# Cosine attention and a gated product: bank rotation of the projection, an earlier first projection, and held norms

## The chip, the cores and the metric

The kernel runs on one core of a Trainium2 chip. The metric is the device time of one execution in microseconds (us). The kernel before has a median of 431.3 us in 11 runs (429.36 to 435.12).

The core has five engines with a queue each. TensorE (PE) does the matmuls and the transposes by matmul; PEld is its weight load. VectorE (DVE), ScalarE (ACT) and GpSimd (POOL) work on tiles. SyncE (SP) issues most DMA transfers. An engine takes its queue in order, and engines wait for each other by semaphores.

## The reference

Inputs are q, k and v, each 8 batches x 12 heads x 448 positions x 64 values in float32, a scalar tau of 0.1, and two weight matrices, w_in (768 x 2048) and w_out (2048 x 768).

```
q_n = q / (norm(q) + 1e-6);  k_n = k / (norm(k) + 1e-6)      # norm over the 64 values of a position
attn = softmax(q_n @ k_n.T / tau)                            # 448 x 448 for each batch and head
x = (attn @ v), heads side by side                           # 3584 x 768
h = x @ w_in                                                 # 3584 x 2048
out = (h * cos(h)) @ w_out                                   # 3584 x 768, float32
```

## The kernel before

**Tiles.** A *pair* is two heads of one batch; the kernel counts 48 pairs g, six to a batch. A *unit* u is three pairs, half a batch, and is what one load brings: raw q and k into `raw`, v into `vin`, both in two alternating buffers. For each unit the kernel squares the raw values (L727, on POOL or ACT; for unit 2 and some pairs of units 0 and 1 the sums come from batch-norm statistics, L736), sums them on DVE (`reduce`, L756), takes the reciprocal root with ln and exp on ACT (`rnorm`, L784 and L787; a Newton iteration on POOL for unit 2), and scales q and k on POOL (L795), giving `qks`. v is copied to bf16 with a column of ones (`copy_v`: on DVE for units 0 and 1, on POOL, L705, for the rest).

For each pair, `qks` is transposed to `qkT`: by PE for the first 12 pairs (L827), by DMA on SP for the others (L814). Then come the scores (L845: per step two matmuls, one for each head, side by side in the array), their exponential on ACT (L850) into `PX`, the attention step (L868: 32 matmuls of 65 columns into the bank pair AV), and on DVE the reciprocal of the row sum and the product with it (L878 `rcp`, L879 `xs`). `xs` is transposed to `xT`, by DMA (L885) or by PE (L898).

For each batch, the *projection* `m1` computes h in eight steps gi. A step is two tiles of 128 x 448 in one pair of banks, 12 matmuls of L917 (two tiles x six pairs c of xT). ACT takes the cosine (L931), DVE multiplies it with h into `gT` (L933). The *second product* (L966) multiplies gT by w_out, 16 matmuls of 384 columns into one bank (PO or PO2), copied out by DVE (L975) and written by DMA. It has no place of its own: its matmuls are cut into small groups that fill PE between the scores and the attention steps of the next batch.

**Banks.** There are three pairs of banks, called AV, SC0 and SC1, and two single ones, PO and PO2. Scores, projection and attention share the three pairs. Which pair step gi of a projection takes stands in `TURN = (1, 2, 0, 1, 2, 0, 1, 0)` (L614; 0 is AV, 1 is SC0, 2 is SC1): SC0, SC1, AV, SC0, SC1, AV, SC0, AV. The last batch's projection gets a turn of its own (L1175).

**Early tiles.** In batch 0 the first two steps of the projection (`early` = 2) are split: `split` is the number of pairs c that the early part covers. It is five, so the early part needs xT of pairs 0 to 4, and the sixth pair follows later.

**Order.** The kernel first records every operation with its reads and writes, then a planner (`arrange`, `play`) lays them out in time with assumed costs and due times (`late`, plus a `bias` for an operation), and `emit` writes each engine's queue in the planned order, with semaphore waits. `order_only(a, b)` demands only that b starts behind a on the same engine. Stream A of PE (scores, attention, projection) keeps its order nearly; stream B (the second product) fills gaps. Where the plan has a gap on PE that is long enough, in the warm-up and later, `emit` puts in matmuls on zeros into PO or PO2 (L1010), which compute nothing that is used. In the plan PE's and SP's queues begin at 0.7 us and the others at 0.

**Norms in time.** `norms(u, p)` (L1024) is called ahead of the pairs that need it; the norms of an even unit u from 6 on fall into the time of the projection of batch u/2 - 2, and those of odd units come soon behind. `project` (L1092) calls the projections of batches 1 to 6; batch 0's is at L1142 and batch 7's at L1175.

Of the kernel before, what the change touches and what calls it, by code (L numbers as in the profile page):

```python
# [6 lines left out]
ACT = mybir.ActivationFunctionType  # L7
# [7 lines left out]
    "sq": ["BA", "BA", "P", "BP", "P", "P"],  # L15
    "scale": ["DD", "P", "P", "P", "P", "P"],
}


DEBUG = 0  # L20
# [9 lines left out]
class Program:  # L30
# [24 lines left out]
    def op(self, eng, fn, reads=(), writes=(), cost=0.0, mode=None, dma=None, bulk=0.0, lock=False, label="", bias=0.0,  # L55
           stream="A"):
        o = Op()
        o.eng, o.fn, o.dma, o.cost, o.mode, o.bulk, o.lock = eng, fn, dma, cost, mode, bulk, lock
        o.label, o.idx, o.inc, o.count, o.late, o.bias, o.free = label, len(self.ops), False, None, None, bias, self.free
        o.stream, o.group = stream, self.group if self.group is not None and not self.free else -1 - o.idx  # L60
        deps = {}
        for t in reads:
            w = self.writer.get(t)
            if w is not None:
                deps[w.idx] = (w, True)
        for t in writes:
# [12 lines left out]
        self.ops.append(o)  # L79
        return o  # L80
# [47 lines left out]
    def rehearse(self, factor, first, rounds=4):  # L128

        ops = sorted(self.ops, key=lambda o: (o.start, o.idx))  # L130
        streams = {}
        for o in ops:
            streams.setdefault(o.eng, []).append(o)
        jobs = self.queues()
        took = {o.idx: o.end - o.start for e in jobs for o in jobs[e]}
        for n in range(rounds):
            start, end = {}, {}
            free = {e: 0.0 for e in streams}
            free["PE"] = free["SP"] = 0.7
            at = {e: 0 for e in streams}  # L140
            port, mode = 0.0, None
            for _ in ops:
                best = None
                for e in streams:
                    if at[e] == len(streams[e]):
                        continue
                    o, r = streams[e][at[e]], free[e]
                    for y, k in o.deps:
                        if y.idx not in start:
                            break  # L150
                        r = max(r, start[y.idx] if k is None else end[y.idx] + self.latency(y, o))
# [66 lines left out]
    def play(self):  # L218
# [6 lines left out]
            for y, k in o.deps:  # L225
                users[y.idx].append((o, k))
        free = {e: 0.0 for e in self.ENGINES}
        free["PE"] = free["SP"] = 0.7
        mode, port = None, 0.0
        queue, clock = {"SP": [], "ACT": [], "POOL": []}, [0.0]  # L230
        self.gaps = []
# [102 lines left out]
        while todo or any(queue.values()):  # L334
            best = None
            for e in self.ENGINES:
# [5 lines left out]
                else:  # L342
# [4 lines left out]
                    o = min((o for o in waiting[e] if ready_at[o.idx] <= now + self.look), key=lambda o: (o.late, o.idx))  # L347
# [8 lines left out]
            s, _, o, grp = best  # L356
# [133 lines left out]
def bass_cosine_attention__then__act_gcu_kernel(  # L490
# [9 lines left out]
    B, NH, S, D = q.shape  # L500
# [3 lines left out]
    UP = 3  # L504
# [7 lines left out]
    NKC = DM // 128  # L512
    NF = FF // 128
# [7 lines left out]
    APART = 2 * PB  # L521
    NO = 4
    GATE = "T12"
    BEHIND = "sq0.2"
    NEWTON, STEPS, STEPSON = (2,), 3, "P"
    BN, BNU = 0.128, (2,)
    BU = "BP"
    N2 = ((0, 1), (1, 3))
    SQ2 = "PPP"
    CUT = 640  # L530
    SOON = -4.0
    BYHEAD = False
    BEHIND0 = "sq0.2"
    LASTW = "scale1.2"
    BEFORE2 = None
    G3 = 12
# [366 lines left out]
        if g >= 2 * PB - 1:  # L903
            m2_emit(max(0, len(m2_queue) - KEEP[g // PB - 1]))

    def m1(b, early=0, split=NKC, turn=TURN):
        table(SINSET)

        def names(gi):
            return [PHs[turn[gi]][0]]  # L910

        def step(gi, a, c0, c1):
            n, ph = 2 * gi + a, PHs[turn[gi]][1]

            def f(e):
                for c in range(c0, c1):
                    t = e.matmul(ph[:, a, 0:S], W1v[:, c, 128 * n : 128 * n + 128], xTv[b % 2][:, c, :],  # L917
                                 start=(c == 0), stop=(c == NKC - 1))
                return t

            P.op("PE", f, [("W1", n * NQ1 // NF)] + [("xT", b % 2, c) for c in range(c0, c1)], names(gi), cost=(c1 - c0) * MM,
                 mode="F", label="M1 %d.%d" % (b, n))

        for gi in range(early):
            for a in range(2):
                step(gi, a, 0, split)
        for gi in range(NF // 2):
            ph, cz = PHs[turn[gi]][1], gi % 2
            for a in range(2):
                step(gi, a, split if gi < early else 0, NKC)  # L930
            act(lambda e, ph=ph, cz=cz: e.activation(cosv[cz], ph[:, :, 0:S], ACT.Sin, bias=cst.ap()[:, 0:1], scale=1.0),  # L931
                names(gi) + ["cst0"], [("cos", cz)], 2 * S, "S", 1, label="sin%d.%d" % (b, gi))
            dve(lambda e, ph=ph, cz=cz, gi=gi: e.tensor_tensor(  # L933
                gTv[:, 2 * gi : 2 * gi + 2, S * (b % 2) : S * (b % 2) + S], ph[:, :, 0:S], cosv[cz], ALU.mult),
                names(gi) + [("cos", cz)], [("gT", b % 2, gi)], 2 * S, label="g%d.%d" % (b, gi))
        table(EXPSET)
# [84 lines left out]
    def find(label):  # L1021
        return [o for o in P.ops if o.label == label][-1]

    def norms(u, p, p1=UP):  # L1024
        if u >= NU:
            return
        if u < 2:
            heads = ((0,), (1,)) if (u, p) == (0, 0) and BYHEAD else ((0, 1),)
            how = PLAN["sq"][UP * u + p]
            if how[0] == "B":  # L1030
                moments(u, p, how)
            else:
                square(u, p, how, heads)
                reduce(u, p, heads)
            rnorm(u, p, p + 1)
            scale(u, p, PLAN["scale"][UP * u + p])
            return
        for x in range(p, p1):
            if u in BNU:
                moments(u, x, BU)  # L1040
                continue
            square(u, x, SQ2[x] if u == 2 else "A" if u in (3, 4, 5) and x == 2 else "P")
            reduce(u, x)
        rnorm(u, p, p1)
        for x in range(p, p1):
            scale(u, x, "P")
# [44 lines left out]

    def project(b, g):  # L1092
        first = len(P.ops)
        m1(b)
        if g in DEFER:
            norms(g // UP + 1, 0)
            for x in range(g + 3, g + 4 + AT1):
                transposes(x)
        first = [o for o in P.ops[first:] if o.eng == "PE"][0]
        for u in (2 * b + 4, 2 * b + 5):  # L1100
            if u < NU:
                load(u, 0, UP)
# [17 lines left out]
    copy_v(1)  # L1120
    for g in range(PB):
        pair(g)
    P.order_only(find(BEHIND0), find("W1.0"))
    P.order_only(find(BEHIND), find("W1.1"))
    last_scale = find(LASTW) if LASTW else None
    for p in range(UP):
        load(2, p, p + 1)
# [11 lines left out]
    load_w2(3)  # L1139
    load_v(3)  # L1140
    attend(PB - 1)
    m1(0, 2, NKC - 1)  # L1142
    copy_v(2)
    P.free = False
    banks[0] = [("PO", PO.ap()), ("PO2", PO2.ap())]
    for p, p1 in N2:
        norms(2, p, p1)
        for g in range(PB + p, min(PB + p1, PB + 2)):
            transposes(g)
    m2_add(0)  # L1150
# [21 lines left out]
                project(g // PB - 1, g)  # L1172
    attend(NG - 1)
    m2_emit()
    m1(B - 1, 2, UP, (2, 0, 1, 2, 0, 1, 2, 0))  # L1175
    m2_add(B - 1)
    banks[0] = banks[0] + [(n, x[:, 0, :]) for n, x in PHs]
    m2_emit()
# [37 lines left out]
```

## Time and profile before

| | |
|---|---|
| median of 11 runs | 431.3 us |
| the profiled execution, its own time | 430.06 us |
| its span, first to last instruction | 428.2 us |
| TensorE busy (matmul) | 418.9 us, 98% of the span |
| ScalarE busy | 260.4 us, 61% |
| VectorE busy | 222.6 us, 52% |
| GpSimd busy | 194.4 us, 45% |
| matmuls of the second product into PO (L966) | 152.3 us |
| matmuls of the projection into SC and AV (L917) | 95.0 + 58.5 us |
| matmuls on zeros (L1010), 50 of them | 13.8 us |

The projections start at 36.46, 89.92, 141.19, 190.81, 240.33, 289.92, 339.48 and 383.94 us. What lies between two of them is called the stretch of the earlier batch: its second product, with the scores and the attention of what comes next.

In the timeline a row is start, duration, engine, line, operation, tiles and count; brackets hold the idle time just before and what ended it. A matmul's duration includes its latency, so durations on PE overlap. In the chain of work that ended last the pieces don't overlap, and their starts can be subtracted. A page's names leave buffer numbers out: SC is SC0 or SC1, PO is PO or PO2.

### The profile page before, as it was taken

The numbers are of one execution on the slowest core, as the hardware profiler recorded it, in microseconds if no ns is written. First come the engines' busy times: TensorE is split into PE (matmuls) and PEld (weight loads), VectorE is DVE, ScalarE is ACT, GpSimd is POOL, SyncE is SP. The second block draws the span as 40 slices with busy tenths as digits, with TensorE's granted clock in tenths as the row PEclk, the third lists the DMA queues.
The fourth block names the chain that finished last, engine by engine and source line by source line (L and its number), as shares of the span: only waits on it lengthen the run. The fifth ranks groups of instructions, "written<-read, shape, count | busy, mean of one in ns | idle before, by whom it ended". The sixth has DMA issues, their size and how long they took to land.

```text
span 428.2 us, 8988 instructions
## 1 busy us (share of the span) xinstructions
PE 418.9 (98%) x3798; PEld 230.4 (54%) x3798; DVE 222.6 (52%) x403; ACT 260.4 (61%) x316; POOL 194.4 (45%) x147
## 2 busy tenths in 40 slices
PE   8899999998999999999999999999999999999997
PEld 3355455554555555555455545555555555555565
DVE  6987786365536476334943367334863353334422
ACT  2895488874676647684676646765576746754400
POOL 3875499624666559711883158810786100000000
DMA  8999997597299896549875494548946301220023
GB/s 242 265 235 225 241 253 161 123 240 170 63 183 236 180 266 142 124 108 231 167 123 130 119 273 110 124 92 200 235 93 121 84 0 39 60 60 0 13 77 97
DMA packets 92008, 63.19 MB, mean 148 GB/s; under 512 B 52288, under 2 KB 86976, under 8 KB 91968
## 3 DMA queue, kind: packets, MB, share of 16 engines
q1 hardware_dynamic: 87312, 55.47, 56.9%
q0 software_dynamic: 3680, 6.29, 7.9%
q10 hardware_dynamic: 976, 0.86, 0.7%
q8 instruction: 30, 0.49, 0.5%
q14 instruction: 10, 0.08, 0.1%
HBM read 45.61 MB, written 11.01 MB: 132 GB/s over the span
## 4 chain that ended last, share of the span: by engine, by line
PE 89%; ACT 3%; POOL 3%; DVE 3%; DMA 1%; issue 1%; POOLq 0%; DVEq 0%; ACTq 0%
PE PO L966 32%; PE SC L917 21%; PE AV L917 13%; PE AV L868 11%; PE SC L845 5%; PE AV L845 3%; ACT PX L850 3%; POOL qks L795 2%; PE SC L966 1%; PE AV L966 1%; DVE st L736 1%; DMA raw<-in_q_dram 1%; POOL sq L727 1%; PE PO L827 1%; PE PO L898 1%
## 5 line engine op out<-in xcount | busy, mean ns | idle before, releaser
L966 PE MATMUL PO<-W,gT 128*128 128x384 bf16 x832 | 152.3, 327 | 0.1
L850 ACT ACTIVATE PX<-SC 112x896 bf16<-112x896 f32 x144 | 123.4, 916 | 3.1 <-PE SC L845 2.7
L966 PEld LDWEIGHTS PO<-W,gT 128*128 128x128 bf16 x832 | 74.1, 98 | 62.5 <-issue 18.6
L727 POOL TENSOR_TENSOR sq<-raw 112x1024 bf16<-112x1024 f32 x39 | 73.1, 1893 | 73.6 <-DMA raw<-in_q_dram 73.6
L917 PE MATMUL SC<-xT,W 128*128 128x448 bf16 x480 | 95.0, 352 | 0.0
L795 POOL TENSOR_TENSOR qks<-raw,rn 112x1024 bf16<-112x1024 f32 x47 | 88.4, 1901 | 10.7 <-ACT rn L787 10.5
L850 ACT ACTIVATE PX<-AV 112x896 bf16<-112x896 f32 x48 | 44.0, 917 | 47.8 <-PE AV L845 47.8
L931 ACT ACTIVATE cosb<-SC,cst 128x896 f32<-128x896 f32 x40 | 40.2, 1007 | 50.4 <-PE SC L917 50.4
L917 PEld LDWEIGHTS SC<-xT,W 128*128 128x128 bf16 x480 | 46.3, 98 | 42.2
L933 DVE TENSOR_TENSOR gT<-SC,cosb 128x896 bf16<-128x896 f32 x40 | 43.5, 1090 | 45.0 <-ACT cosb L931 44.8
L917 PE MATMUL AV<-xT,W 128*128 128x448 bf16 x288 | 58.5, 352 | 1.8 <-ACT cosb L931 1.1
L868 PEld LDWEIGHTS AV<-va,PX 112*128 112x128 bf16 x1536 | 49.6, 97 | 14.7 <-ACT PX L850 11.4
L868 PE MATMUL AV<-va,PX 112*128 112x65 bf16 x1536 | 56.0, 193 | 0.7 <-ACT PX L850 0.2
L756 DVE TENSOR_REDUCE n<-sq 112x16 f32<-112x1024 bf16 x42 | 50.8, 1212 | 10.2 <-POOL sq L727 9.4
L975 DVE COPY osb<-PO 128x384 f32<-128x384 f32 x52 | 28.8, 554 | 47.6 <-PE PO L966 47.6
L845 PE MATMUL SC<-qkT 64*128 64x448 bf16 x288 | 42.2, 352 | 1.7 <-DVE qkT L835 0.7
L931 ACT ACTIVATE cosb<-AV,cst 128x896 f32<-128x896 f32 x24 | 24.2, 1007 | 32.0 <-PE AV L917 31.8
L917 PEld LDWEIGHTS AV<-xT,W 128*128 128x128 bf16 x288 | 27.6, 98 | 29.5 <-issue 3.1
L878 DVE RECIPROCAL rcp<-AV 112x8 f32<-112x8 f32 x48 | 9.9, 207 | 63.7 <-PE AV L868 63.6
L705 POOL CAST va<-vin 112x1536 bf16<-112x1536 f32 x14 | 20.5, 1463 | 44.1 <-PE AV L868 35.4
L933 DVE TENSOR_TENSOR gT<-AV,cosb 128x896 bf16<-128x896 f32 x24 | 26.2, 1090 | 15.7 <-ACT cosb L931 15.3
L879 DVE TENSOR_TENSOR xs<-AV,rcp 112x512 bf16<-112x512 f32 x48 | 33.2, 692 | 2.1
(50 smaller groups left out, 180.9 us busy)
## 6 DMA issues: line engine op xcount, KB each, us to landing
vin<-in_v_dram SPq DMA_DIRECT2D x16, 672.0 KB, 8.8
raw<-in_k_dram SPq DMA_DIRECT2D x12, 672.0 KB, 7.8
raw<-in_q_dram SPq DMA_DIRECT2D x12, 672.0 KB, 10.2
W<-in_moe_w_in_dram POOLq DMA_DIRECT2D x2, 1536.0 KB, 21.2
W<-in_moe_w_out_dram POOLq DMA_DIRECT2D x4, 768.0 KB, 21.1
raw<-in_k_dram SPq DMA_DIRECT2D x12, 224.0 KB, 6.8
out_dram<-osb SPq DMA_DIRECT2D x7, 336.0 KB, 2.8
out_dram<-osb SPq DMA_DIRECT2D x8, 288.0 KB, 2.7
```

The costliest lines, as they stand in the source:

```text
L727: pool(lambda e, x=x, y=y: e.tensor_tensor(y, x, x, ALU.mult), src_, dst, 0.1 + n * 1.78e-3, label=name)
L756: dve(lambda e, o=o, hs=hs: e.tensor_reduce(out=n2v[i][:, o, :], in_=sqv[p][:, hs[0] : hs[-1] + 1, :, :], axis=mybir.AxisListType.X, op=AL ...
L795: f = lambda e, s0=s0, s1=s1: e.tensor_tensor(qksv[i][:, p, s0:s1, :, :].rearrange("p s h d -> p h s d"), rawv[i][:, h, s0:s1, :], bass.AP ...
L845: t = e.matmul(bank[:, a, 0:S], qkT[k].ap()[r, NP * c : NP * c + 128], qkT[k].ap()[r, S : 2 * S], start=True, stop=True)
L850: act(lambda e: e.activation(PXv[j][:, c, 0 : 2 * S].rearrange("p (a s) -> p a s", a=2), bank[0:NP, :, 0:S], ACT.Exp, scale=1.0 / TAU), [n ...
L868: t = e.matmul(AVv[:, a, DV * x : DV * x + n], PXv[j][:, c, k : k + 128], vav[i][:, NJ * (2 * p + a) + c, 0:n], start=(c == 0), stop=(c == ...
L879: dve(lambda e: e.tensor_tensor(xsv[y].rearrange("p x h d -> p h x d"), AXv[:, :, :, 0:D], bass.AP(rcp[y], 0, [[NS, NP], [NJ, 2], [1, NJ], ...
L917: t = e.matmul(ph[:, a, 0:S], W1v[:, c, 128 * n : 128 * n + 128], xTv[b % 2][:, c, :], start=(c == 0), stop=(c == NKC - 1))
L931: act(lambda e, ph=ph, cz=cz: e.activation(cosv[cz], ph[:, :, 0:S], ACT.Sin, bias=cst.ap()[:, 0:1], scale=1.0), names(gi) + ["cst0"], [("c ...
L933: dve(lambda e, ph=ph, cz=cz, gi=gi: e.tensor_tensor(gTv[:, 2 * gi : 2 * gi + 2, S * (b % 2) : S * (b % 2) + S], ph[:, :, 0:S], cosv[cz], ...
L966: r = e.matmul(po[:, 0 : w1 - w0], gTv[:, y, col : col + 128], W2v[:, y, w0:w1], start=(y == 0), stop=(y == NF - 1))
L975: dve(lambda e, po=po, o=o, w0=w0, w1=w1: e.tensor_copy(osb[o].ap()[:, w0:w1], po[:, 0 : w1 - w0]), keys, [("osb", o, w0)], w1 - w0, label ...
```

## The change

- `project` calls `m1` with the turn `TURN[:-1] + (2,)`: in batches 1 to 6 the eighth step goes into SC1, not AV. Batch 0 keeps `TURN`.
- `split` becomes a tuple. For batch 0 it is (0, 4, 5): the two early steps run with pairs 0 to 3 first, then with pair 4; pair 5 follows as before. For batch 7 it is (0, 3), which is what it was.
- For even units u from 4 on, `norms` puts each `reduce` behind the last product (`g...`, step 7) of batch u/2 - 2, by `order_only` on DVE.
- The V copy of unit 3 (`va3`) gets 8 us on its due time in the planner, so that POOL may take other work first.
- In the plan, ACT's queue begins at 0.7 us.
- `BEHIND` becomes a tuple with the values that stood there, and `XS5` is off: neither changes anything.

The planner runs anew over all operations, so the queues are cut a little differently in many places.

```diff
+BIAS = {"va3": 8.0}
...
+        o.bias += BIAS.get(label, 0.0)
...
-            free["PE"] = free["SP"] = 0.7
+            free["PE"] = free["SP"] = free["ACT"] = 0.7
...
+    SPLIT = (0, NKC - 2, NKC - 1)
...
+    HOLD = True
...
-    def m1(b, early=0, split=NKC, turn=TURN):
+    def m1(b, early=0, split=(0,), turn=TURN):
...
         for gi in range(early):
-            for a in range(2):
-                step(gi, a, 0, split)
+            for c0, c1 in zip(split, split[1:]):
+                for a in range(2):
+                    step(gi, a, c0, c1)
...
-                step(gi, a, split if gi < early else 0, NKC)
+                step(gi, a, split[-1] if gi < early else 0, NKC)
...
+        late = [o for o in P.ops if o.label == "g%d.%d" % (u // 2 - 2, NF // 2 - 1)] if HOLD and u >= 4 and u % 2 == 0 else []
         for x in range(p, p1):
...
             reduce(u, x)
+            for y in late:
+                P.order_only(y, P.ops[-1])
...
-        m1(b)
+        m1(b, turn=TURN[:-1] + (2,))
...
-    m1(0, 2, NKC - 1)
+    m1(0, 2, SPLIT)
...
-    m1(B - 1, 2, UP, (2, 0, 1, 2, 0, 1, 2, 0))
+    m1(B - 1, 2, (0, UP), (2, 0, 1, 2, 0, 1, 2, 0))
```

More of the change, by code (lines that the diff above doesn't have):

```diff
@@ L227, in play @@
         free = {e: 0.0 for e in self.ENGINES}
-        free["PE"] = free["SP"] = 0.7
+        free["PE"] = free["SP"] = free["ACT"] = 0.7
         mode, port = None, 0.0
@@ L523, in bass_cosine_attention__then__act_gcu_kernel @@
     GATE = "T12"
-    BEHIND = "sq0.2"
+    SPLIT = (0, NKC - 2, NKC - 1)
+    BEHIND = ("sq0.2", "sq0.2")
     NEWTON, STEPS, STEPSON = (2,), 3, "P"
@@ L527, in bass_cosine_attention__then__act_gcu_kernel @@
     BU = "BP"
+    XS5 = False
+    HOLD = True
     N2 = ((0, 1), (1, 3))
@@ L532, in bass_cosine_attention__then__act_gcu_kernel @@
     BYHEAD = False
-    BEHIND0 = "sq0.2"
     LASTW = "scale1.2"
@@ L1122, in bass_cosine_attention__then__act_gcu_kernel @@
         pair(g)
-    P.order_only(find(BEHIND0), find("W1.0"))
-    P.order_only(find(BEHIND), find("W1.1"))
+    for x, y in enumerate(BEHIND):
+        P.order_only(find(y), find("W1.%d" % x))
     last_scale = find(LASTW) if LASTW else None
@@ L1147, in bass_cosine_attention__then__act_gcu_kernel @@
         norms(2, p, p1)
+        if p == 0 and XS5:
+            P.order_only(find("xs5"), [o for o in P.ops if o.label == "bn2.0"][0])
         for g in range(PB + p, min(PB + p1, PB + 2)):
```

## The prediction

> **What bounds the kernel now.** I read the page's busy shares first, then the busy time by stretches, then the order of events on PE and VectorE around each projection, then the front.
>
> ```profile
> PE 418.9 (98%) x3798; PEld 230.4 (54%) x3798; DVE 222.6 (52%) x403; ACT 260.4 (61%) x316; POOL 194.4 (45%) x147
> ```
>
> TensorE is busy 98% of 428.2 us and no other engine over 61%. Its work is fixed by the algorithm, so time comes only from microseconds in which PE waits, or does work that computes nothing. The zero matmuls of L1010 are such work; they count as busy. By stretches (columns: from:to, length, then busy us and count of PE, PEld, DVE, ACT, POOL, the clock, DMA share, GB/s):
>
> ```profile
> 89.90:109.40 19.50, 18.35 (x98) 9.35 (x97) 13.34 (x14) 9.72 (x10) 7.47 (x5) 1.00 0.75 173
> 190.80:209.20 18.40, 18.30 (x98) 9.31 (x96) 11.04 (x12) 8.76 (x9) 5.59 (x3) 1.00 1.03 216
> ```
>
> Both are a whole projection of one batch (96 matmuls of L917); the first, batch 1, is 1.1 us longer for the same work. Its cause stands in the order of events on PE and then on VectorE (start, duration, engine, line; in brackets the idle time before):
>
> ```profile
> 103.45 2.43 PE L917 MATMUL SC<-xT,W 128*128 128x448 bf16 x12
> 107.03 2.43 PE L917 MATMUL AV<-xT,W 128*128 128x448 bf16 x12 [1.15 <-ACT cosb L931]
> ...
> 104.67 1.22 DVE L756 TENSOR_REDUCE n<-sq 112x16 f32<-112x1024 bf16 x1 [1.09 <-POOL sq L727]
> 105.81 1.08 DVE L933 TENSOR_TENSOR gT<-AV,cosb 128x896 bf16<-128x896 f32 x1
> ...
> 204.29 2.43 PE L917 MATMUL SC<-xT,W 128*128 128x448 bf16 x12
> 206.83 2.43 PE L917 MATMUL AV<-xT,W 128*128 128x448 bf16 x12
> ```
>
> The last pair of tiles goes into AV, whose previous tiles are only two places back. It waits until cosine and product have read AV. In batch 1 a reduction stands in front of that product. The wait is put down to the cosine, which had ended at 104.72 (103.71 + 1.01); the late event is the product, ended at 106.89. In later batches (204.29 to 206.83 = 2.54 us for a step of 2.27) 0.27 us are lost. The front:
>
> ```profile
> 1.62 9.36 PE L1010 MATMUL PO<-zt 128*128 128x448 bf16 x34 [1.62 <-DVE zt L1009]
> 10.82 0.79 PE L827 MATMUL PO<-ident,qks 112*128 112x112 bf16 x8
> ...
> 33.93 1.11 PE L1010 MATMUL PO<-zt 128*128 128x448 bf16 x5
> 35.12 0.37 PE L898 MATMUL PO<-ident,xs 112*128 112x112 bf16 x4
> 35.33 1.13 PE L868 MATMUL AV<-va,PX 112*128 112x65 bf16 x32
> 36.30 2.06 PE L917 MATMUL SC<-xT,W 128*128 128x448 bf16 x10
> ```
>
> At 33.93 PE does five zero matmuls while pair 4 is normalised; the projection could have used that time.
>
> **What the Trainium skill says.** "TensorE: Matmul & The Clock Gate", Back-to-back issue gap: a warm matmul takes N/2.4 ns plus 2.5, so 189 ns for 448 columns and 162.5 for 384. The trace agrees (2.27/12 and 2.60/16 us), and I use these. The same page, What's actually happening: a cold PE runs at half clock. The trace shows the first fifteen or so zero matmuls 0.373 us apart, and 0.19 from 7.2 us on. "PSUM — Partial Sum Buffer", Engine vs sequencer instructions: VectorE's queue is strict FIFO and matmuls run in program order, so a reduction ahead of a product holds PE up as batch 1 shows.
>
> **The change part by part** (orders are those of the built program).
>
> *Plain rotation, six projections.* The last tile pair moves from AV to SC1, last used three places back. The projection of the last batch (383.94 to 402.36) already rotates so: its eight steps follow without a gap, 18.42 us with 0.2 of transposes inside. The chain has batch 1 from 89.92 to 109.46 = 19.54, batches 2 to 6 at 18.48 (141.19 to 159.67), 18.45, 18.46, 18.49 and 18.45. Eight steps of 2.27 are 18.16. So batch 1 gains 1.38 and the five others 1.53. What becomes late next is SC1 for the first scores behind: sine and product of the last tile end 2.22 us after the projection (209.26 to 211.48). PE now has 12 matmuls of the second product (1.95) and two score steps (0.1 + 0.19 + 0.19) first: 2.43. It fits by 0.2. Without that cover the loss is up to 0.5 a batch.
>
> *Split at four and five pairs (batch 0).* Eight matmuls (1.51 us) move ahead of pair 4's transposes, in place of five zero ones. From the last attention step (33.98) to the end of the projection (55.08) were 21.10 us; the wait of 1.14 to 35.12 and 0.17 of re-entry go: -1.31. xs of pair 4 is ready at 35.06, before the eight end (35.5), and xs of pair 5 about 1.0 us behind its attention, when 6 matmuls have run. Bounds -1.3 and 0: it can be handed back behind 55 us (first rival). Batch 0 keeps its old rotation, so its 0.27 stays.
>
> *ACT's queue counted from 0.7 us in the planner.* The built front has 37 zero matmuls instead of 34. Three more at 0.19 are 0.57. The first half of qks becomes ready about when the 34 end (PE loads its weights at 10.64), the second at 11.19. With 37 the transposes start at 11.39 instead of 10.82, so the second copy of qkT (L835) ends about 12.47 instead of 12.04: +0.43. The chain runs on through reduction, ln, rn and the scale at 12.93 with no slack to 35.12, so I take all of it. Bounds 0 and +0.6.
>
> *V copy of unit 3 behind its scales.* The built POOL order has this copy where it was, ahead of the three scales: the part does nothing. Copy at 62.15 to 63.62, scale at 64.06 behind rn: it cost nothing anyway. 0.
>
> *Norms held behind the products (units 6, 8, ... 14; unit 4's product, of batch 0, is long done by then).* Three reductions of 1.21 us move from between the products to behind the last. Nothing waits on them early: unit 8's first scale slips from 162.8 to about 173.5 (rn now comes after the third group of scores, and the V copy stands first on POOL, waiting for the attention that ends at 171.9). Six scales of 1.88 then end near 184.8; unit 8's first transpose leaves near 175.4 and lands 3.4 later, against scores at 188.3. SP's transposes behind it slip alike; xT of pair 22 (normalised near 180.5) leaves about 181, needed at 190.8. The raw buffers come free by 184.8, and the loads into them wait for the projection at 190.8 anyway. The danger is rcp and xs (L878, L879): in the built order two reductions and a copy stand between the last product and rcp. From the end of the projection: product 2.22, reductions and copies to about 5.2 (batch 2) or 6.0 (later); the attention step ends near 5.2. xs then ends near 7.0, and the next scores wait for it; in front of them stand 12 matmuls now, instead of 8, to 7.15. So hidden: 0. If the cover fails, up to 0.3 in each of five batches, +1.5. Below nothing there is no gain beyond the rotation's.
>
> *The planner's re-cut.* Four second-product matmuls move from batch 1's stretch into batch 0's, and four from batch 2's to the end; the total stays. Batch 0's stretch has 17 runs of scores instead of 18 (0.29 for a run of one step against 0.19: with the re-entry, 0.2): -0.2. In batch 1's stretch two visits stand 8 matmuls apart plus one zero one; three exponentials take 2.64 (380.21 to 382.76), 0.67 of scores and 1.30 of matmuls and 0.1 fill 2.07: wait about 0.45. Sum +0.25, bounds -0.6 (waits of batch 0's stretch that go) and +1.0. The last attention step waited for exponentials (382.80, 0.3 us); 16 matmuls now stand there instead of 12: -0.3, or 0.
>
> **Sum**: -1.38 - 1.53 - 1.31 + 0.43 + 0.25 - 0.3 = -3.84 us. The profiled execution took 430.06 (span 428.2 and 1.86 around it), 1.2 under the median of 431.3; so span 424.4 (428.2 - 3.84), and the median becomes 427.5.
>
> **Rivals.** *The front's gain is handed back.* Batch 0's stretch is paced by things that do not move: the last quarter of w_out, the V load landing at 62.15 with its copy on POOL before unit 3's scales, ACT at 30.36 of 34.80 us. Then -1.31 + 0.43 goes: -2.96, 428.3. For it: the chain passes through PX and qks there. Against: its waits are short, and I find four more matmuls of filler done by then.
>
> *The held norms surface in part.* 0.6 us in each of five batches, half a reduction: +3.0, so -0.84, 430.5, no difference. For it: VectorE's order has them directly before rcp. Against: the planner's matmuls in front of the scores.
>
> *Slower.* Place: rcp and xs behind the attention step after each of five projections. If a whole reduction (1.21) stands uncovered, +6.05: 433.5. It decides once the next scores start more than 0.77 us later than in the sum; slower by half a per cent needs 1.20. Against: 1.95 us of matmuls cover it.
>
> **How the numbers follow.** Forecast 0.62, front handed back 0.16, part surfacing 0.13, slower 0.06, the rest (a larger gain, 425) 0.03. Half a per cent (2.16 us) is about what a measurement can tell: faster 0.79, no difference 0.15, slower 0.06. The unknowns give about 1.5 us to either side of the forecast; the range reaches up to the middle of the second rival, 425.4 to 430.4.
>
> **What would show it.** In the profile after: no [..] wait on L917 in any projection from batch 1 on, and each 18.2 us; no zero matmuls at 34 us and L917 there; 37 at the front and the first transposes at 11.4; first projection ending about 54.2; batch 1's starting about 89.3, batch 2's about 139.0. I am wrong if scores (L845) wait for xs (L879) or PE for cosb behind projections, or if stretches between projections exceed 31.2 us.

## The result and the profile after

The changed kernel takes 428.06 us, the median of 13 runs (426.95 to 429.55), against 431.37 us in 48 runs of the kernel before beside it. The ratio is 0.9925, with a 95% interval from 0.9905 to 0.9945: 3.3 us faster. The forecast was 427.5 us in a range from 425.4 to 430.4. The profiled execution took 426.95 us, its span is 425.1: 3.1 us less than before, where the sum had 3.84.

The page's busy shares of the changed kernel:

```profile
PE 417.4 (98%) x3797; PEld 231.1 (54%) x3797; DVE 221.9 (52%) x403; ACT 260.3 (61%) x316; POOL 194.7 (46%) x147
```

PE is as full as it was, and busy 1.5 us less. Its busy time by stretches (columns as before: from:to, length, then busy us and count of PE, PEld, DVE, ACT, POOL, the clock, DMA share, GB/s), for projections 1 and 3:

```profile
89.40:107.60 18.20, 18.20 (x98) 9.44 (x97) 10.80 (x11) 9.67 (x10) 6.99 (x5) 1.00 0.82 211
187.80:206.00 18.20, 18.20 (x98) 9.39 (x96) 8.54 (x9) 8.79 (x9) 5.60 (x3) 1.00 0.96 241
```

Both projections fill their stretch: batch 1's no longer stands out. The order of events on PE at the front, around projection 1 and behind projection 3 (L921 is the projection, L849 the scores, L971 the second product, L1015 the zero matmuls):

```profile
1.63 9.55 PE L1015 MATMUL PO<-zt 128*128 128x448 bf16 x37 [1.63 <-DVE zt L1014]
11.01 0.56 PE L831 MATMUL PO<-ident,qks 112*128 112x112 bf16 x8
...
34.23 1.67 PE L921 MATMUL SC<-xT,W 128*128 128x448 bf16 x8
...
100.58 2.43 PE L921 MATMUL AV<-xT,W 128*128 128x448 bf16 x12
102.85 4.70 PE L921 MATMUL SC<-xT,W 128*128 128x448 bf16 x24
107.39 2.11 PE L971 MATMUL PO<-W,gT 128*128 128x384 bf16 x12
...
207.90 0.36 PE L849 MATMUL AV<-qkT 64*128 64x448 bf16 x2
208.09 0.66 PE L849 MATMUL SC<-qkT 64*128 64x448 bf16 x4
```

The eight projection matmuls stand at 34.23, in the place of the five zero ones. The last two steps of projection 1 are one group of 24 into SC, with no bracket. The last row looks harmless, and is a cost that the sum had missed: four score matmuls take 0.66 us there, and 0.54 in nearly all other places.

Differences of starts in the chain give the stages. The last column is what the prediction's terms come to for each.

| stage, us | before | after | difference | in the sum |
|---|---|---|---|---|
| start to the end of projection 0 | 55.08 | 54.24 | -0.84 | -0.88 |
| stretch behind it | 34.84 | 35.13 | +0.29 | +0.45 |
| projection 1 | 19.54 | 18.18 | -1.36 | -1.38 |
| projections 2 to 6 | 92.33 | 91.09 | -1.24 | -1.53 |
| stretch behind projection 1 | 31.73 | 31.54 | -0.19 | -0.20 |
| stretch behind projection 2 | 31.14 | 30.55 | -0.59 | -0.65 |
| stretches behind projections 3 to 5 | 93.27 | 93.61 | +0.34 | 0 |
| from the end of projection 6 | 70.27 | 70.76 | +0.49 | +0.35 |
| span | 428.20 | 425.10 | -3.10 | -3.84 |

The places are right, and 0.74 us are missing, mostly in the projections and in the stretches behind 3 to 5. Two rows need a word. The first stage came out as forecast by luck: the split brought some 0.4 us less than the sum had, and raw data that came earlier made up for it (see the zero matmuls and the split). And of the 0.29 us that are missing in projections 2 to 6, half is a matter of counting: the sum set eight bare steps, 18.16, against lengths in the chain, and in the chain a changed projection measures 18.19. The other half is a wait of 0.15 us ahead of projection 4, which the chain counts into it (18.34); a second profile of the same program does not have it.

### The profile page after: what moved, and what is told of

The parts are those of the page before. It is cut to its first block, busy times and chain, and to the rows that moved or that the text cites. A ratio compares the mean times of both kernels' runs of the same rounds, so it can differ in the third digit from the quotient of the medians.

```text
span 425.1 us, 8980 instructions
## 1 busy us (share of the span) xinstructions
PE 417.4 (98%) x3797; PEld 231.1 (54%) x3797; DVE 221.9 (52%) x403; ACT 260.3 (61%) x316; POOL 194.7 (46%) x147
## 3 DMA queue, kind: packets, MB, share of 16 engines
HBM read 45.61 MB, written 11.01 MB: 133 GB/s over the span
## 4 chain that ended last, share of the span: by engine, by line
PE 81%; DMA 8%; ACT 5%; POOL 4%; DVE 1%; issue 0%; SPq 0%; ACTq 0%; POOLq 0%
PE PO L971 28%; PE SC L921 22%; PE AV L872 10%; PE AV L921 8%; PE SC L849 5%; DMA W<-in_moe_w_out_dram 4%; DMA vin<-in_v_dram 4%; PE AV L849 3%; ACT PX L854 3%; PE PO L1015 2%; POOL qks L799 2%; ACT L644 2%; PE SC L971 1%; ACT cosb L936 1%; PE AV L971 1%; POOL sq L731 1%
## 5 line engine op out<-in xcount | busy, mean ns | idle before, releaser
L971 PE MATMUL PO<-W,gT 128*128 128x384 bf16 x832 | 152.0, 327 | 0.0
L921 PE MATMUL SC<-xT,W 128*128 128x448 bf16 x552 | 108.8, 352 | 0.0
L971 PEld LDWEIGHTS PO<-W,gT 128*128 128x128 bf16 x832 | 74.3, 97 | 61.2 <-issue 18.4
L936 ACT ACTIVATE cosb<-SC,cst 128x896 f32<-128x896 f32 x46 | 46.2, 1007 | 57.3 <-PE SC L921 57.3
L938 DVE TENSOR_TENSOR gT<-SC,cosb 128x896 bf16<-128x896 f32 x46 | 50.1, 1091 | 57.3 <-ACT cosb L936 57.2
L921 PEld LDWEIGHTS SC<-xT,W 128*128 128x128 bf16 x552 | 53.3, 98 | 48.9 <-DVE xT L906 0.2
L849 PE MATMUL SC<-qkT 64*128 64x448 bf16 x288 | 42.8, 352 | 1.9 <-DVE qkT L839 0.8
L921 PE MATMUL AV<-xT,W 128*128 128x448 bf16 x216 | 44.0, 352 | 0.1
L921 PEld LDWEIGHTS AV<-xT,W 128*128 128x128 bf16 x216 | 21.0, 98 | 19.9 <-issue 0.5
L936 ACT ACTIVATE cosb<-AV,cst 128x896 f32<-128x896 f32 x18 | 18.1, 1008 | 21.8 <-PE AV L921 21.6
L938 DVE TENSOR_TENSOR gT<-AV,cosb 128x896 bf16<-128x896 f32 x18 | 19.6, 1090 | 17.0 <-ACT cosb L936 16.9
```

What stands on the lines that cost most here:

```text
L849: t = e.matmul(bank[:, a, 0:S], qkT[k].ap()[r, NP * c : NP * c + 128], qkT[k].ap()[r, S : 2 * S], start=True, stop=True)
L938: dve(lambda e, ph=ph, cz=cz, gi=gi: e.tensor_tensor(gTv[:, 2 * gi : 2 * gi + 2, S * (b % 2) : S * (b % 2) + S], ph[:, :, 0:S], cosv[cz], ...
L971: r = e.matmul(po[:, 0 : w1 - w0], gTv[:, y, col : col + 128], W2v[:, y, w0:w1], start=(y == 0), stop=(y == NF - 1))
```

## Experiments

Eleven more kernels ran, and the changed one once more, four at a time on one chip, with 6 to 22 runs of each. A measure that the times alone don't give comes from their profiles. From the start of projection 1 to the end of the span, eight profiles whose programs differ only ahead of it take the same to 0.3 us; the start of projection 1 itself moves by 2.5 us among them. The table splits each profiled span there.

| run | median us | ratio to before, 95% | start of projection 1 | from there to the end |
|---|---|---|---|---|
| before | 431.37 | | 89.84 | 338.4 |
| changed kernel | 428.06 | 0.9925 (0.9905 to 0.9945) | 89.23 | 335.9 |
| changed kernel again | 428.24 | 0.9926 (0.9903 to 0.9950) | 91.72 | 335.9 |
| rotation alone | 429.46 | 0.9950 (0.9932 to 0.9968) | 92.75 | 337.9 |
| rotation undone | 430.68 | 0.9959 (0.9941 to 0.9977) | 89.81 | 337.9 |
| hold off | 429.05 | 0.9935 (0.9911 to 0.9959) | 90.77 | 337.1 |
| reduction twice | 429.78 | 0.9961 (0.9939 to 0.9982) | 90.09 | 337.2 |
| split undone | 429.54 | 0.9941 (0.9921 to 0.9961) | 90.89 | 335.8 |
| 34 zero matmuls | 428.15 | 0.9913 (0.9895 to 0.9932) | 90.76 | 335.9 |
| V copy behind scales | 427.89 | 0.9910 (0.9887 to 0.9933) | 90.39 | 335.7 |
| V load halved | 427.27 | 0.9883 (0.9845 to 0.9921) | 89.72 | 335.8 |
| V load halved, split undone | 428.44 | 0.9909 (0.9877 to 0.9941) | 90.72 | 335.9 |
| unit 4 later | 428.24 | 0.9902 (0.9865 to 0.9940) | 90.94 | 335.9 |
| unit 4 later, V copy behind | 427.13 | 0.9880 (0.9843 to 0.9918) | 88.69 | 336.7 |

The chips differ (before: 431.3 to 432.4 us), so medians are compared within a group of four, and ratios across groups; 0.001 is 0.43 us. One group is rotation alone, rotation undone, split undone and 34 zero matmuls; one is the changed kernel again, hold off, reduction twice and V copy behind scales; one is the last four rows.

### The rotation alone, and undone

```
 rotation alone (kernel before):  -        m1(b)
                                  +        m1(b, turn=TURN[:-1] + (2,))
 rotation undone (changed kernel):-        m1(b, turn=TURN[:-1] + (2,))
                                  +        m1(b)
```

> The kernel before with the plain rotation in projections 1 to 6 and nothing else of the change; the planner cuts the rest anew (4 second-product matmuls go from the fourth stretch to the end, the total is the same; one run of scores more in the stretch behind projection 0). Theory (the bank two places back is the cause of every wait in those projections, also of the 1.15 us in batch 1): all six projections at 18.2 us, so -1.34 in batch 1 and -0.26 in each of the five others, with +0.2 for the run of scores -2.4 in all: profile near 427.6, time 0.994 to 0.995 of before. Rival A (batch 1's 1.15 us belong to the reduction in front of the product, and only holding the norms takes it away): projection 1 stays near 19.4 and the gain is about -1.1. Rival B (without the hold the reductions between the products make the first scores behind the projection wait for the last product's bank instead): projections at 18.2 but the stretches behind them 0.3 to 1.2 longer each, gain -1 to 0 or a loss.

> The changed kernel with the old rotation in projections 1 to 6; everything else as changed, norms held too (4 second-product matmuls move from the second stretch to the seventh by the planner, one zero matmul more). Theory: six waits of 0.27 us come back, +1.6 us: profile near 428.6; projection 1 at 18.45 as the others, for the held reduction no longer stands in front of the product. Rival (rotation alone cured batch 1, the hold had no part in it): projection 1 back at 19.5, +2.7 us, profile near 429.7.

With the rotation alone all six projections take 18.16 us by the timeline, 0.26 less than five of them took, and 1.3 less for projection 1. But behind projection 1 PE now waits: PE, and then VectorE, in the timeline of the rotation alone:

```profile
113.16 0.35 PE L845 MATMUL SC<-qkT 64*128 64x448 bf16 x2
114.94 0.37 PE L845 MATMUL SC<-qkT 64*128 64x448 bf16 x2 [1.43 <-DVE gT L933]
...
112.59 1.21 DVE L756 TENSOR_REDUCE n<-sq 112x16 f32<-112x1024 bf16 x1
113.71 1.08 DVE L933 TENSOR_TENSOR gT<-SC,cosb 128x896 bf16<-128x896 f32 x1
```

Without the hold, reductions stand between the products. The last product, into SC1's tile, starts at 113.71, 2.80 us behind the projection's end (110.91), and the scores that need SC1 wait 1.43 us. That is rival B, in one batch; in the four stretches behind (31.13 to 31.30) it is not there, and one of them waits 0.48 us for xs. So in this execution batch 1's 1.15 us were not taken away by the rotation: it moved them from the projection to the scores. The times don't show that this is the rule. The profiled execution took 432.49, the slowest of the 20 runs, and their median lies 2.7 us below the kernel before on the same chip, where theory had 2.4.

With the rotation undone and the norms held, projection 1 takes 18.42 (89.81 to 108.23), as the others do: theory right, rival out. So the hold alone removes batch 1's 1.1 us from the projection, and the rotation 0.26 us from each. The score groups tell what the rotation costs in return. The rows of the kernel with the rotation undone, behind projection 3:

```profile
211.06 0.36 PE L849 MATMUL AV<-qkT 64*128 64x448 bf16 x2
211.25 0.54 PE L849 MATMUL SC<-qkT 64*128 64x448 bf16 x4
```

0.54 us in all six batches, as in the kernel before; 0.66 in all six of the changed kernel. The third score step needs SC1. In the changed kernel the last product, into SC1's tile, ends at 208.24 (207.15 + 1.09), and a score starts some 0.15 us behind the product it waits for (114.79 to 114.94 above), so at 208.39; its turn came at 208.28. PE waits 0.11 us by this working, and the group is 0.12 longer. The stretches agree: behind projections 3 to 5, with the same 112 second-product matmuls in both, 31.10 with the rotation undone and 31.23 with it (31.38 once, with the wait ahead of projection 4). The plain rotation brings 0.26 - 0.12 = 0.14 us a batch by the stages, not 0.3.

In time, undoing the rotation costs more than six times 0.14. From the start of projection 1 on it is 2.0 us, and the median lies 2.5 above that of the kernel with 34 zero matmuls, the nearest to the changed one on this chip; theory had 1.6, the rival 2.7. Most of the rest lies in the stretch behind projection 1: 32.18 us, with four second-product matmuls fewer than the changed kernel's 31.56. PE waits there 0.76 us for an xs that stands behind reductions of squares whose data landed at 129.91. Two runs below, hold off and the last one, have the new rotation and the same wait (0.98 and 0.81), so a late load is the likelier cause; that the rotation has no part in it isn't shown. By the stages, then, the rotation is worth 0.8 us with the norms held. By the ratios it is 1.5 from this run, and 2.2 from the rotation alone, where batch 1's wait counts with it; the intervals reach 0.8 or more to either side.

### The hold off, and its danger priced

```
 hold off:         -    HOLD = True
                   +    HOLD = False
 reduction twice, in reduce(), for even u >= 6 and p == 0:
                   +    e.tensor_reduce(out=<a buffer that nothing reads>, in_=<the same squares>, ...)
```

> The changed kernel without the hold on the norms: reductions stand between the products again; per stretch as many second-product matmuls and scores as in the changed kernel, one zero matmul fewer. Theory, from the run with the rotation alone, where the scores behind projection 1 waited 1.43 us for the last product and behind the later projections not at all: the hold is worth 1.0 to 1.4 us, all of it in the stretch behind projection 1 (31.6 to 32.6 or more), and nothing in the four behind it. Rival A (the hold is worth nothing beyond the rotation, as the sum had it): all stretches within 0.1. Rival B (the held reductions in front of rcp cost): 0.1 to 0.3 faster in each of five stretches.

> The changed kernel with the first of the three held reductions done twice in units 6, 8, 10, 12 and 14 (the first time into a buffer that nothing reads; 1.21 us more on VectorE ahead of rcp, five times; not known to the planner, so every order is the same). Theory, from the changed kernel's profile (xs ends at 114.74, 163.58, 212.79, 262.26 and 311.72; the scores behind it start at 115.28, 163.85, 213.23, 262.78 and 312.17; 0.2 to 0.4 us of VectorE's idle time lies between): xs is 0.8 to 1.0 later, and the scores wait for it by 0.57, 0.6, 0.4, 0.4 and 0.4: +2.3 us. Rival (more cover than these starts show, since PE waits for exponentials behind anyway): under 0.5 in all.

Hold off: 337.1 us from the start of projection 1 on against 335.9, and 0.8 us in the medians of the group, which these runs can't tell from nothing. The stretch behind projection 1 is 32.30 against 31.80 in the repeat of the changed kernel, but that is another wait: for xs, behind squares whose load landed at 130.74. The score wait came one batch later. PE and VectorE in its timeline, the last row being the late product:

```profile
161.63 0.35 PE L849 MATMUL SC<-qkT 64*128 64x448 bf16 x2
162.83 0.36 PE L849 MATMUL SC<-qkT 64*128 64x448 bf16 x2 [0.85 <-DVE gT L938]
...
156.22 1.22 DVE L760 TENSOR_REDUCE n<-sq 112x16 f32<-112x1024 bf16 x1 [1.25 <-POOL sq L731]
...
161.61 1.08 DVE L938 TENSOR_TENSOR gT<-SC,cosb 128x896 bf16<-128x896 f32 x1
```

In this execution the square for the first reduction came at 156.2 (its load had landed at 154.22), and the products queued behind it were late; that stretch is 0.68 us longer, the three behind it are the same (31.23 in the repeat too). The theory had the mechanism and the wrong batch. In the two profiles with the new rotation and no hold, one batch each paid 0.7 and 1.4 us, the batch whose square came late. How often that happens in the other runs isn't shown.

Reduction twice: the stretches behind projections 1 to 5 are longer by 0.38, 0.40, 0.21, 0.21 and 0.21 us against the changed kernel's 31.57, 30.58, 31.23, 31.23 and 31.23 (the shorter of its two profiles each time): 1.41 in all, where theory had 2.3 and the rival under 0.5. The medians of the group differ by 1.54. So 1.21 us more ahead of `rcp` cost 0.2 to 0.4 each: the cover of xs is 0.8 to 1.0 us, thin but enough. That prices the two rivals with held norms surfacing: they needed 0.6 or 1.21 us uncovered, and behind the projections of the changed kernel nothing is.

### The zero matmuls and the split

```
 34 zero matmuls: -        free["PE"] = free["SP"] = free["ACT"] = 0.7
                  +        free["PE"] = free["SP"] = 0.7
 split undone:    -    SPLIT = (0, NKC - 2, NKC - 1)
                  +    SPLIT = (0, NKC - 1)
```

> The changed kernel with the planner's count for ACT's queue at zero again: the only difference in the program is 34 zero matmuls at the front in place of 37. Theory (the transposes behind them have their data earlier and wait for the zero matmuls alone): first transposes at 10.65 instead of 11.01 us, first projection ends 0.36 earlier, profile near 426.6. Rivals: the first transposes wait for qks at 10.9 anyway (gain 0.1 at most), or the gain is handed back behind the projection (0).

> The changed kernel with the first tiles of batch 0 split at five pairs only; five zero matmuls stand at 34 us again, and three in the stretch behind. Theory (the eight matmuls fill time in which nothing else can run, and the gain is kept to the end): first projection ends near 55.5 instead of 54.24, +1.3 us, profile near 428.2. Rival (the front's gain is handed back, because w_out, the V load and its copy pace the stretch behind): the end of the projection is late by as much, but that stretch is shorter by 0.6 or more, and the total rises by 0 to 0.7.

With 34 zero matmuls the transposes start at 10.67, as theory had it, and then nothing shows: the transposes behind projection 0 start at 54.05 against 54.08, and the ratios (0.9913 and 0.9925) lie within each other's intervals. The chains of this kernel and of the changed one show why:

```profile
8.91 2.31 DVE qks L799 x2
11.22 0.05 issue
11.27 0.38 PE PO L831 x4
11.65 0.02 issue
11.68 0.39 DVE qkT L839
```

```profile
1.63 9.55 PE PO L1015 x37
11.18 0.21 PE PO L831 x4
...
11.41 0.69 DVE qkT L839 x2
```

With 34 the second half of qks is ready at 11.22, behind the zero matmuls, and its copy ends at 12.07. With 37 the raw data came 0.43 us earlier (4.21 against 4.64), qks was ready at 10.88, and its transposes waited for the zero matmuls; the copy ended at 12.10. That the two ends agree is chance: each execution waits for the later of the two, data or zero matmuls.

The distance from qks to the end of the copy tells which. It is 0.85 or 0.86 us in the three profiles with 34 zero matmuls, and in five of the eleven with 37: there three more cost nothing. In the other six it is longer, by 0.37 in the changed kernel's first profile. Three matmuls at 0.19 can make up 0.57 of such a wait at most. And what follows does hang on this copy: in seven of the ten profiles with the split, the projection's first matmuls start 22.12 to 22.14 us behind its end. (In the other three the copy ends early, at 11.03 to 11.33, and they start 23.0 to 23.6 behind.) So three zero matmuls cost 0 to 0.6 us, an estimate from these waits, according to when the data come and when TensorE comes to speed; the times don't show it.

The split undone puts the transposes behind projection 0 at 55.59 (and at 55.31 in a run below), against 53.88 to 54.46 in the ten with the split: 1.2 us between the means. Part of this is the front. From the end of that copy it is 42.88 to 42.94 us in the four profiles without the split and 41.97 to 41.99 in the seven with it, so the split itself is worth 0.9 to 1.0, not the 1.3 of the sum. In the ratios 0.7 us of it are left against the changed kernel, and 1.4 in the medians against the kernel with 34 zero matmuls on the same chip. These times can't tell whether any of it is handed back; the next runs look at the place.

### What sets the start of projection 1

The changed kernel itself started projection 1 at 89.23 in its first profile and at 91.72 in its second:

> The changed kernel once more, on the same chip as the three that follow, for comparison and for a second look at its first 90 us. In the profiles so far all stages behind the second projection repeat to 0.02 us from one kernel to another, while the start of projection 1 lies anywhere from 89.2 to 92.8 us. Theory (the first 70 us are paced by transfers, 230 to 240 GB/s without a pause, and how fast they run differs from one execution to the next): the same program shows another landing of the V load of unit 3 than 62.47 us, and projection 1 starts later by what that landing is later. Rival (the differences came from the edits): 62.5 and 89.2 again, to 0.2.

The chain of the first profile, and then that of the second:

```profile
27.65 18.71 DMA W<-in_moe_w_out_dram
...
46.79 15.68 DMA vin<-in_v_dram
62.47 0.05 issue
62.52 1.47 POOL va L709
63.99 1.87 POOL qks L799
```

```profile
27.96 20.60 DMA W<-in_moe_w_out_dram
...
49.00 15.96 DMA vin<-in_v_dram
64.96 0.05 issue
65.01 1.47 POOL va L709
66.48 1.87 POOL qks L799
```

A piece of w_out lands, which lets SP issue the V loads; V of unit 3 lands 16 us later; POOL copies it, and only then scales unit 3, for which PE waits (0.29 us in the first profile, 1.19 in the second). From the landing to projection 1 there are 26.76 us in both, and in four more kernels with this front, to 0.02. Of the 2.49 us between the landings 1.89 are this piece of w_out, for the same bytes; 0.28 are the V load, and 0.31 a later issue. The theory holds: in these kernels the start of projection 1 is set by a transfer, the edits have little part in it, and the first profile, the fastest of its 13 runs, was a lucky one. Without the split it is different: there the load landed at 63.07 and projection 1 started 27.82 behind it, at 90.89, 35.3 behind the end of projection 0. So the split's gain reaches projection 1 when the load lands early, and is lost when it lands after 64.1 or so (90.89 - 26.76, an estimate).

```
 V copy behind scales, after the planning: + find("va3").start = find("scale3.2").start + 0.001
 V load halved (unit 3):                   three of six heads are loaded
 unit 4 later, after the planning:         + after(find("load u4 p0"), find("load v u2"))
```

> The changed kernel with one instruction moved, after the planning: the V copy of unit 3 on POOL stands behind the three scales of its unit, as the change's words say; the queues of the other engines are the same, instruction for instruction. Theory (the V load lands last of the first transfers, at 62.5 to 65.3 us in four looks, POOL holds the scales behind its copy, and PE waits 0.3 to 1.4 us for the first of them): the scales start when rn is there, no wait of PE for qks in that stretch, which is then 34.8 us or less whenever the load lands; 0.4 to 1.2 us faster than the changed kernel. Rivals: rn is no earlier than the copy's end, or the load of w_out paces the stretch (0.8 us of wait for it in one look) - then the gain is 0.3 at most; or values wait for the late copy (unit 3's first attention step stands near 75 us, the copy would end near 69.6) - then a loss.

> The changed kernel with one transfer halved: the V load of unit 3 brings three of its six heads (336 KB in place of 672; the other three are computed from an older load, so this leaves part of the input out); all queues are the same. In five profiles of kernels with the changed front, projection 1 starts 26.76 us behind the landing of that load, to 0.02 (62.47 to 89.23, 63.99 to 90.75, 64.96 to 91.72, 64.01 to 90.77, 63.33 to 90.09). Theory (this landing paces the changed kernel): it comes about 1.4 us earlier (336 KB at 240 GB/s), and projection 1 with it, down to a floor near 88.9: 0.5 to 1.4 us faster than the changed kernel. Rival (the landing only goes along with something else that is late, the load of w_out or the keys and queries of unit 3): under 0.4.

> The same halved transfer, with the first tiles of batch 0 split at five pairs only. With the whole transfer the split's gain was 1.5 us at the end of projection 0, but the times differ by 0.7 us or so. Theory (the rest is handed back to that landing in most executions): with the landing earlier, projection 1 starts a fixed 35.3 us behind the end of projection 0 (90.9 here against 89 to 89.5 with the split), and the times of this pair differ by 1.3 to 1.9 us. Rival (the split is worth 0.7 us whatever the transfers do): 0.4 to 1.0.

> The changed kernel with one wait more: SP issues the loads of unit 4's keys and queries once the V load of unit 2 has landed (59.7 to 62.1 us) and not as soon as their buffers are free (55.7); the order of every queue is the same. Theory (these 1.34 MB take their share of the transfers from 56 us on, in front of the V load of unit 3, which PE waits for first): that load lands 1 to 2.5 us earlier, 59.5 to 62.5, and projection 1 starts 26.76 behind it or at its floor near 88.9, so 0.4 to 1.4 us faster. Rivals: transfers are served in the order of their issue, and nothing changes; or the loads of unit 4, which landed near 71 and were needed near 71 to 73, are late, and PE waits for the scales of unit 4: 0.5 to 2 us slower.

> Both edits, the later loads of unit 4 and the V copy of unit 3 behind its scales, on the changed kernel. Theory: the scales of unit 3 start with rn, which needs the keys and queries of unit 3 alone (landed near 56), and the V copies are no longer late: projection 1 starts at 88.5 to 89.5 whatever the transfers do, 0.7 to 1.6 us faster than the changed kernel. Rivals: as for each of the two, a loss of 0.5 to 2 us by unit 4's late loads, or no difference.

V copy behind scales: PE's wait for qks is gone, and the scales start at 64.05, behind `rn`, which itself came late in this execution (63.97, against 62.45 in the changed kernel's first profile). The medians differ by 0.35 us, too little to be told from nothing; projection 1 started at 90.39. Other transfers come next: PE waited 0.7 us for the V copy of unit 2 and 0.4 for w_out.

V load halved: no wait for qks either. The chain starts with another transfer,

```profile
29.24 30.04 DMA W<-in_moe_w_out_dram
59.33 0.82 PE PO L971 x4
```

a piece of w_out that PE waited 0.94 us for. Projection 1 starts at 89.72, not at the floor of 88.9. The median is 1.0 us below that of the next kernel on the same chip, unit 4 later, which runs as the changed one does: within what theory had. With the split undone as well it is at 90.72, 35.41 behind the end of projection 0, and the list of PE's waits in that stretch is empty. The pair differs by 1.17 us in the medians and 1.00 in the start of projection 1, where the transposes behind projection 0 differ by 1.11. That is between the two expectations, and about what the split is worth at its place. With the V load out of the way the split's gain arrives whole. How much of it is lost with the whole load is not shown by the times, which gave 0.7 and 1.4.

Unit 4 later changes nothing that shows: V of unit 3 landed at 64.14 and projection 1 started 26.80 behind it. The theory on the shared transfers falls, as far as one profile tells. With the V copy behind the scales added, the median is 427.13 against 428.24 on the same chip, and all six of its times lie below five of the other's six. POOL's timeline, of the kernel with unit 4 later, and of the one with both edits:

```profile
64.19 1.47 POOL L709 CAST va<-vin 112x1536 bf16<-112x1536 f32 x1 [0.73 <-DMA vin<-in_v_dram]
65.61 5.63 POOL L799 TENSOR_TENSOR qks<-raw,rn 112x1024 bf16<-112x1024 f32 x3
```

```profile
62.33 5.62 POOL L799 TENSOR_TENSOR qks<-raw,rn 112x1024 bf16<-112x1024 f32 x3 [1.63 <-ACT rn L791]
67.89 1.46 POOL L709 CAST va<-vin 112x1536 bf16<-112x1536 f32 x1
```

The scales now wait for `rn` and for no V load, and projection 1 starts at 88.69, the earliest of all. (Transfers also ran faster in that execution: `rn` was there at 62.25, in the other at 64.65.) It loses 0.81 us of this in the stretch behind, waiting for xs. Its ratio of 0.9880 is the lowest of the kernels that compute everything. It is 1.1 us ahead of unit 4 later on the same chip; that it is ahead of the changed kernel is not shown, since the intervals of their ratios overlap.

## Why the prediction was right, and where it was not

- **Plain rotation, six projections** (-2.91). The place was right: in the changed kernel no wait stands inside a projection from batch 1 on. In the projections it measured -2.60. Two steps failed. "It fits by 0.2" for SC1 behind the projection: it misses by 0.11, and costs 0.12 in each of six batches, 0.7 us in all. The 2.43 us of PE's work in front were right. The 2.22 us for sine and product were short: they count from 209.26, where the chain ends the projection, while PE begins what follows at 209.09. From there the product ends 2.39 later, and the score starts 0.15 behind it. And "batch 1 gains 1.38" by the rotation: in the one profile with the rotation alone, 1.1 of it only moved to the scores. The two parts are not a sum. Together they take the wait away, and each alone takes another share of it.
- **Norms held** (0, danger +1.5). Right that `rcp` and xs are covered: in the changed kernel no score waits for xs behind a projection, and an added 1.21 us costs 0.2 to 0.4. Too low on the gain: "below nothing there is no gain beyond the rotation's" is wrong. The hold was worth 0.7 and 1.4 us in the two profiles without it, since with it the product that the next scores need is not behind a reduction that waits for a late load.
- **Split** (-1.31). The place is right, and the size was 0.9 to 1.0. The eight matmuls start 0.44 us behind the start of the last attention matmuls before them (33.79 to 34.23), where the zero ones started 0.26 behind (33.67 to 33.93). The remaining 0.2 is near the 0.17 of re-entry that the sum took off; that this did not go is likely, and not shown. The first rival, that the V load and its copy take the gain back, was given 0.16 and is half true: with the split, the start of projection 1 is the landing plus 26.76 us. An early landing let the profiled execution keep all that the sum had (89.23 against 89.3 forecast).
- **Zero matmuls** (+0.43). "The chain runs on with no slack to 35.12" was right. What failed is to take two instants of one execution as fixed, that of the data and that at which TensorE comes to speed. The 37 took 0.19 us longer than the 34 had, not 0.57, since the speed came at 6.5 us and not at 7.2; the transposes started at 11.01 and not at 11.39. And qks was ready at 10.88 and not at 11.19. So the copy ended at 12.10, against 12.04 before: 0.31 gained by the data, 0.37 lost to the zero matmuls. The loss is near the forecast, but in the second profile it is 0. In the stage table this early data hides the split's error: -1.31 + 0.43 forecast, -0.90 + 0.06 measured.
- **V copy of unit 3** (0). As forecast, the built program has it where it was, and so that part of the change does nothing. But "it cost nothing anyway" held for the kernel before, where `rn` came later than the copy's end; in the changed one it holds the scales for up to 1.2 us of PE's time.
- **Re-cut** (+0.25 and -0.3). Right within 0.16 us a stage, the zero matmul and the short wait at 133 us with it.
- **The signs.** As forecast, no score waited for xs behind a projection, and PE for no cosine. "Stretches between projections exceed 31.2" was no good sign: the sum itself makes 31.53 of the stretch behind projection 1, and it measured 31.54.

The forecast of the time came out 0.6 us low; in the profile the SC1 wait and the projections' 0.3 account for what is missing. That it came so near is partly luck. What the hold brings stood under the rotation, and the profiled execution had early data, which hid what the split lacked, and an early landing.

## What to carry to other kernels

A bank moved away from a wait has a next reader: count both times from the same instant, to a tenth of a microsecond, with the step from one engine to the next in the sum, and treat a slack of 0.2 us as a coin toss that is thrown once and paid in each repetition. Two edits at one wait are not a sum: ask of each what it does alone, here a bank that is late because of a product, and a product that is late because of a reduction. And before an earlier start is counted as a gain, look for the transfer that the next stage waits for, in more than one execution.

## What the runs showed of the hardware that was not expected

- The time of the same transfers differs from one execution to the next by more than most of the edits are worth: V of unit 3 landed at 62.47 and at 64.96 us in two profiles of one program, while 215 to 263 GB/s were moved in each of the six slices that make up the first 64 us of their pages. The time from projection 1 to the end repeated to 0.3 us where no load was late.
- The 37 zero matmuls at the front took between 8.48 and 10.09 us in eleven executions, 34 of them 8.33, 8.88 and 9.36. The matmuls go from 0.37 us apart to 0.19 at different instants, 4.5 to 7.6 us, and three matmuls more or less (0.57 us) are lost in that.
